# Where in a group of blocks the weight rounding stands: all of the group, or its first five sixths

## The chip, the cores and the metric

The program runs on one core of one Trainium2 chip. A core has five engines that work side by side, each through its own queue in order: TensorE (PE in the profile; its weight loads, which overlap its multiplications, are PEld), VectorE (DVE), ScalarE (ACT), GpSimd (POOL) and SyncE (SP), which here only issues transfers. The metric is the device time of one execution in microseconds (us), as the median of several runs. The kernel before took 2952.58 us (five runs, 2948.7 to 2953.84).

## The reference

```python
def _attn_ref(x, filt_r, filt_i):              # x: (8, 3008, 256)
    X = np.fft.rfft(x, axis=1)
    Y = X * (filt_r + 1j * filt_i)[None, :, :]
    return np.fft.irfft(Y, n=x.shape[1], axis=1).astype(np.float32)

def _moe_ref(x, w_gate, w_val, w_out):         # x: (24064, 256), d_ff = 1536
    g = x @ w_gate
    silu = g * (1.0 / (1.0 + np.exp(-g)))
    return (silu * (x @ w_val) @ w_out).astype(np.float32)
```

A filter in the frequency domain along the sequence is followed by a gated feed-forward block. The three weight matrices arrive in double precision, and the kernel turns them into single precision itself.

## The kernel before, in words

**Batches, groups, tokens.** The work goes through 8 batches. A batch is cut into 4 chunks of tokens, and the hidden dimension into 3 parts; one chunk with one part is a *group*, so a batch has 12 groups, counted 0 to 11 here. In the first batch groups 0 to 8 go part by part: chunks 0, 1, 2 with part 0, then with part 1, then with part 2. All groups walk through the same hand-written order, `SCHEDULE` (line 85), of 150 *tokens*; the position of a token is its *place*. Every engine takes its instructions in the order in which the tokens issue them. Tokens with a prime belong to the group before.

**What the tokens do.** The products x @ w_gate and x @ w_val are made by a scheme of block combinations. P, Q, A, B and E are products on PE (line 732; `P0` to `P3` and `Q0` to `Q3` with the blocks' own weights, `A01` to `E23` with combined ones). f and c copy a product out of PSUM (ACT, lines 747 and 751), D subtracts two such copies (POOL, `tensor_tensor` of line 228 with D as output), x, s and y combine products (DVE, lines 754 and 232; `x02`, `s12` and `s01` read `D02`, `D12` and `D01`). Of x03, x23 and x02 the s token is a copy on ACT (line 758). m copies (ACT, line 767), e and l go on (ACT line 763, DVE lines 228 and 232), g and u are the silu (ACT, line 774), h and v the product with it (DVE, line 779). The last token of a group, at place 149, is `v03`. S tokens (POOL, lines 225 and 228 with h) combine the hidden values of the group before, W tokens multiply them with the output weights (PE, line 811) and o tokens add the results up (ACT line 822, DVE line 225). t tokens are pieces of the transform of other chunks or of the next batch (lines 548 to 662). n1, n2 and n3 combine or fetch the sums of the next chunk's input blocks. `W2` is the first W token of a group, at place 3; it reads, among others, what `v03` wrote at the end of the group before, and output weights in `wo_t`.

**The preparation of the weights.** It happens once, in the first batch, since the weights are rounded from the raw 64-bit words by integer and floating-point instructions. There are 36 *halves*, each a 256 KB load by SP (line 285) and then (`round_half`, line 287) four DVE instructions (lines 302, 305, 317, 321), four ACT instructions (lines 307, 310, 312, 314) and one to five on POOL (line 329 and four subtractions of line 228 for output weights; lines 341 and 342 and up to two more for the others). After the halves of one part, `combine_weights` (line 351) makes the weights of A, B and E for six pairs, with one instruction on DVE, for some of them one on ACT (line 363), and two on POOL for each (lines 228 and 225 with `wt_t` or, for part 1, `lent`).

`Preparation` (line 378) cuts all of this into 171 *ticks*, numbered 0 to 170. A new half starts nearly every four ticks, and consecutive halves overlap. Within a half the steps come at ticks 0, 1, 2, 3, 4, 6, 7, 9 and 10 from its start: for instance L302 at 0, L305 at 1, L317 at 6, L321 at 7, the multiplication on POOL at 9, what follows it on POOL at 10. Calling `preparation.tick(step)` issues the instructions of the next tick, at this point of the order of every engine. Ticks 0 to 44 are done while the first chunk's transform runs, before group 0. After that the loop of line 1054 calls a tick just ahead of certain tokens:

```python
for place, token in enumerate(SCHEDULE):
    if b == 0 and this and place * TICKS % len(SCHEDULE) < TICKS and \
            (step or place > SCHEDULE.index("A01")):
        preparation.tick(step)
```

`TICKS` is 20 (line 451), so a group has 20 of them, and group 0 only those behind `A01`. At the start of each group `preparation.finish(step)` (line 1045) forces all ticks whose results that group needs: the output weights of part 0 are needed from group 1 on (tick 58 is their last), the weights of part 1 from group 3, those of part 2 from group 6, each with its output weights one group later. Ticks of part 2's weights, from 100 on, may not start before group 3, as they overwrite part 0's.

Of the kernel before, what the change touches and what calls it, by code (L numbers as in the profile page):

```python
# [84 lines left out]
SCHEDULE = """  # L85
# [59 lines left out]
def kernel(  # L145
# [228 lines left out]
    def reload_weights(g, piece):  # L374
        a, b = PIECES[piece]
        tc.keep_in_program_order(nc.sync.dma_start(out=wt_t[:, a:b], in_=w_dram[g, :, a:b]))
# [74 lines left out]
    TICKS = 20  # L451
# [388 lines left out]
    with tc.tile_pool(name="start", bufs=1) as spool0:  # L840
# [47 lines left out]
        for u in range(N_TWO + lag):  # L888
            if u < N_TWO:
                spec.turn(u + 2)  # L890
                step = spec.stage2a(u)
# [60 lines left out]
    def order_of(b):  # L952

        steps = [divmod(step, NG) for step in range(NCHUNK * NG)]
        if b == 0:
            steps[:NT * NG] = [(k, g) for g in range(NG) for k in range(NT)]
        return steps

    def sequence_of(cur, nxt, step):

        steps = order_of(cur.b)
        if step + 1 == len(steps):
            return (lambda d: combine_sequence(nxt.y[0], d)) if nxt else None
        k, after = steps[step][0], steps[step + 1][0]
        if k == after:
            return None
        if cur.b == 0 and NT - 2 < step < NT * NG - 1:
            return lambda d: reload_sums(after, d)
        return lambda d: combine_sequence(cur.y[after], d)

    def sooner(piece):

        for n in range(3):
            next(piece)
            if n == 2:
                next(piece, None)
            yield
# [24 lines left out]
    for b in range(B):  # L1002
        cur, nxt = spec, following if b + 1 < B else None
        spec, following = nxt, Spectral(b + 2)
        plan = [[] for _ in range(NCHUNK * NG)]

        def three(s, k, cur=cur):
            return [s.stage3(k, step) for step in range(4)]

        d = [three(cur, k) for k in range(1, NCHUNK)]  # L1010
        one = [nxt.stage1(u) for u in range(N_ONE)] if nxt else []
        two = []
        for u in range(N_TWO + 2) if nxt else ():
            two += [nxt.stage2b(u - 2)] if u > 1 else []
            two += [nxt.stage2a(u)] if u < N_TWO else []
        if nxt:
            plan[0] = one[0:2] + d[0][0:1] + one[2:3] + d[0][1:2]
            plan[1] = one[3:4] + d[0][2:3] + one[4:5] + d[0][3:4] + one[5:6]
            plan[2], plan[3] = one[6:11], one[11:16]
            plan[4] = d[1] + two[0:1]  # L1020

            plan[5], plan[6] = [iter(())] + two[1:5], two[5:10]
            plan[7] = two[10:11] + d[2]
            plan[8], plan[9] = two[11:16], two[16:21]
            plan[10], plan[11] = two[21:24], three(nxt, 0)
            if b == 0:
                for k in range(NCHUNK - 1):
                    plan[k] = d[k] + one[k:k + 1]
                plan[3], plan[4], plan[5] = one[3:8], one[8:13], one[13:16]
                for n in range(5):  # L1030
                    plan[6 + n] = two[5 * n:5 * n + 5]
                plan[6][0] = sooner(plan[6][0])
        else:
            plan[1], plan[4], plan[7] = d

        for step in range(NCHUNK * NG + (b == B - 1)):
            ghost = step == NCHUNK * NG
            k, g = order_of(b)[min(step, NCHUNK * NG - 1)]
            this = None
            pieces = []  # L1040
            if not ghost:
                pieces = plan[step]
                this = Group(b, k, g, cur.y[k], sequence_of(cur, nxt, step))
                if b == 0:
                    preparation.finish(step)
                chunk = {0: 1, 2: 2, 5: 3}.get(step)
                if b and chunk:
                    for i in range(2):
                        cur.load_t4(chunk, i)
            elif before is None:  # L1050
                break
            ends = {ORDER[e - 1]: n for n, (_, e) in enumerate(PIECES)}
            last = ghost or b == B - 1 and step == NCHUNK * NG - 1
            for place, token in enumerate(SCHEDULE):
                if b == 0 and this and place * TICKS % len(SCHEDULE) < TICKS and \
                        (step or place > SCHEDULE.index("A01")):
                    preparation.tick(step)
                old = token.endswith("'")
                op = token.rstrip("'")
                if op[0] == "t":  # L1060
                    n = int(op[1])
                    ps = pieces_before if old else pieces
                    if n < len(ps):
                        next(ps[n], None)
                elif op[0] in "Wo" or op.endswith(".o"):

                    g0 = older if old else before
                    if g0 is not None and (old or not ghost):
                        g0.project(op)
                else:  # L1070
                    g0 = before if old else this
                    if g0 is not None and not (ghost and op[0] == "S"):
                        g0.step(op)
                if old or this is None:
                    continue
                if nxt and (step, op) == ((4, "P2") if b else (5, "A23")):
                    nxt.load_two(0)
                if b + 2 < B and (step, op) == (9, "B01"):
                    for u in range(2):
                        following.load_x(u)  # L1080
                if nxt and (step, op) == (10, "A12" if b else "E23"):
                    for i in range(2):
                        nxt.load_t4(0, i)
                for f, args in chores.get((step, op), ()) if b == 0 else ():
                    f(*args)
                if op in ends and not last and (b or step >= NT * NG - 1):
                    reload_weights((g + 1) % NG, ends[op])
            older, before, pieces_before = before, this, pieces
# [33 lines left out]
```

## Time and profile before

| | |
|---|---|
| median of five runs | 2952.58 us |
| the profiled execution: its own time | 2952.58 us |
| its span, first to last instruction | 2950.2 us |
| mean granted PE clock | 0.999 |
| busy: PE / PEld / DVE / ACT / POOL | 99% / 95% / 65% / 55% / 54% |
| instructions on PE / DVE / ACT / POOL | 20264 / 4384 / 4208 / 1759 |
| groups 0 to 6 of the first batch (78.4 to 299.8 us): busy PE / DVE / ACT / POOL | 208.7 / 187.6 / 150.7 / 161.9 of 221.4 us |

In the timelines each line gives start and duration in us, the engine, the line of the code, the operation, output and inputs, their sizes and how many instructions the line stands for. A bracket at the end gives how long the engine was idle before it and what released it. Instructions of one engine overlap a little, so starts lie closer together than the durations. In the tables by stretch each engine has its busy time and, in brackets, its instructions; then come the granted PE clock, the DMA engines' busy share and GB/s. A wait for several things is put down to the one that came last.

### The profile page before, as it was taken

To read this page: it belongs to the slowest core of one execution; us is meant where nothing else is said; L and a number is where in the kernel's file an instruction comes from. 1 tells how busy PE (TensorE), PEld (TensorE's weight loads), DVE (VectorE), ACT (ScalarE), POOL (GpSimd) and SP (SyncE) were. 2 spreads that over 40 slices of the span, in tenths; PEclk is the share of its full clock that TensorE was granted. 3 is DMA by queue.
4 is the path that set the end of the run, shared out by engine and by line. 5 is a ranking of instruction groups with operands and counts; after the bars stand their busy time and mean duration, and the time that the engine had idled before them with its cause. 6 is when DMAs were issued, how large, how long until landed. Compare 5 with 4: busy or idle time off the path is not lost.

```text
span 2950.2 us, 57623 instructions
## 1 busy us (share of the span) xinstructions
PE 2913.9 (99%) x20264; PEld 2816.4 (95%) x20264; DVE 1930.8 (65%) x4384; ACT 1610.1 (55%) x4208; POOL 1579.3 (54%) x1759
## 2 busy tenths in 40 slices
PE   7999999999999999999999999999999999999999
PEld 5888999999999999999999999999999999999999
DVE  6888765576655776556765667656666566666666
ACT  6775455555555455555555554555555555555554
POOL 3875654556444655456554556454564545555453
PEclk9999999999999999999999999999999999999999
DMA  8687855575565755566655666556665565644442
GB/s 227 202 265 244 290 193 185 179 222 182 174 189 175 223 191 170 180 193 198 210 159 187 191 199 204 168 175 201 197 197 171 179 206 194 200 138 151 148 130 88
DMA packets 217452, 558.57 MB, mean 189 GB/s; under 512 B 29962, under 2 KB 107642, under 8 KB 217166
## 3 DMA queue, kind: packets, MB, share of 16 engines
q1 hardware_dynamic: 171326, 485.59, 52.2%
q10 hardware_dynamic: 36912, 45.43, 4.5%
q0 software_dynamic: 8928, 23.89, 2.3%
q8 instruction: 162, 2.65, 0.4%
q14 instruction: 124, 1.02, 0.1%
HBM read 459.73 MB, written 95.05 MB: 188 GB/s over the span
## 4 chain that ended last, share of the span: by engine, by line
PE 93%; DVE 1%; DMA 1%; POOL 1%; ACT 0%; issue 0%; SPq 0%; DVEq 0%
PE wa L732 24%; PE wA L811 17%; PE wk L732 16%; PE we L732 12%; PE wG L811 9%; PE wF L811 4%; PE pd L640 3%; PE pa L548 3%; PE pc L620 2%; PE pb L588 2%; DMA lent<-de_tbl 0%; DMA d<-lent 0%; DVE o L225 0%; POOL wt_t L225 0%; DVE pw L317 0%; POOL wt_t L228 0%
## 5 line engine op out<-in xcount | busy, mean ns | idle before, releaser
L732 PE MATMUL wa<-y_t,wt_t 128*128 128x188 f32 x4464 | 880.4, 323 | 5.3 <-issue 1.4
L732 PEld LDWEIGHTS wa<-y_t,wt_t 128*128 128x128 f32 x4464 | 730.0, 190 | 31.0 <-issue 17.3
L225 POOL TENSOR_TENSOR h<-h 128x376 f32<-128x376 f32 x190 | 182.9, 984 | 786.9 <-DVE h L779 767.7
L811 PE MATMUL wA<-wo_t,h 128*128 128x128 f32 x4608 | 577.8, 275 | 3.0 <-DVE o L225 2.0
L811 PEld LDWEIGHTS wA<-wo_t,h 128*128 128x128 f32 x4608 | 563.0, 192 | 16.9 <-issue 10.4
L732 PE MATMUL wk<-y,wt_t 128*128 128x188 f32 x2976 | 568.5, 324 | 0.0
L228 POOL TENSOR_TENSOR h<-h 128x376 f32<-128x376 f32 x570 | 554.4, 994 | 0.5
L732 PEld LDWEIGHTS wk<-y,wt_t 128*128 128x128 f32 x2976 | 479.7, 191 | 25.9 <-issue 19.8
L228 DVE TENSOR_TENSOR we<-we,m 128x376 f32<-128x376 f32 x576 | 318.4, 556 | 197.3 <-PE we L732 138.9
L732 PE MATMUL we<-y_t,wt_t 128*128 128x188 f32 x2232 | 431.5, 323 | 1.4 <-ACT we L763 1.4
L732 PEld LDWEIGHTS we<-y_t,wt_t 128*128 128x128 f32 x2232 | 369.4, 190 | 1.8 <-ACT we L763 1.7
L228 POOL TENSOR_TENSOR D<-f,f 128x376 f32<-128x376 f32 x288 | 280.5, 987 | 104.3 <-ACT f L747 103.3
L232 DVE SCALAR_TENSOR_TENSOR y<-wk,c 128x376 f32<-128x376 f32 x480 | 244.8, 542 | 133.4 <-ACT we L763 82.8
L767 ACT COPY m<-wa 128x376 f32<-128x376 f32 x576 | 272.0, 472 | 88.0 <-PE wa L732 86.8
L774 ACT ACTIVATE g<-wa 128x188 f32<-128x188 f32 x576 | 188.1, 327 | 190.3 <-PE wa L732 182.3
L811 PE MATMUL wG<-wo_t,h 128*128 128x128 f32 x2304 | 288.3, 275 | 0.6 <-DVE o L225 0.6
L811 PEld LDWEIGHTS wG<-wo_t,h 128*128 128x128 f32 x2304 | 281.4, 192 | 0.8 <-DVE o L225 0.8
L774 ACT ACTIVATE u<-we 128x188 f32<-128x188 f32 x576 | 189.0, 328 | 168.8 <-DVE we L228 150.0
L747 ACT ACTIVATE f<-wk 128x376 f32<-128x376 f32 x288 | 139.3, 484 | 235.3 <-PE wk L732 208.0
L751 ACT COPY c<-wk 128x376 f32<-128x376 f32 x288 | 136.0, 472 | 225.3 <-PE wk L732 225.3
L754 DVE SCALAR_TENSOR_TENSOR x<-wk,f 128x376 f32<-128x376 f32 x192 | 104.3, 543 | 235.6 <-PE wk L732 229.9
L763 ACT COPY we<-y 128x376 f32<-128x376 f32 x480 | 224.1, 487 | 33.6 <-DVE h L779 14.8
(142 smaller groups left out, 3914.8 us busy)
## 6 DMA issues: line engine op xcount, KB each, us to landing
wt_t<-w_all SPq DMA_DIRECT2D x174, 896.0 KB
wt_t<-w_all SPq DMA_DIRECT2D x174, 768.0 KB
t<-d SPq DMA_DIRECT2D x62, 384.0 KB
d<-t ACTq DMA_DIRECT2D x112, 192.0 KB
lent<-de_tbl SPq DMA_DIRECT2D x84, 256.0 KB
lent<-in_filt_r_dram SPq DMA_DIRECT2D x336, 64.0 KB
lent<-d SPq DMA_DIRECT2D x84, 256.0 KB
d<-lent ACTq DMA_DIRECT2D x84, 256.0 KB
```

What stands on the lines that cost most here:

```text
L225: return eng.tensor_tensor(out=dst, in0=a, in1=b, op=ALU.add)
L228: return eng.tensor_tensor(out=dst, in0=a, in1=b, op=ALU.subtract)
L232: return nc.vector.scalar_tensor_tensor(out=dst, in0=a, scalar=-1.0, in1=b, op0=ALU.mult, op1=ALU.subtract)
L548: pin(nc.tensor.matmul(out=ps[0:NK], lhsT=wf_t, rhs=self.x.pop(u), start=True, stop=True))
L732: pin(nc.tensor.matmul(out=ps[:, z], lhsT=self.wt[:, SLOT[p], z], rhs=rhs, start=start and z == 0, stop=True, skip_group_check=True))
L747: pin(act.mul(self.small(f"f{i}", f"f{i}", 1), t[f"k{i}"], -1.0))
L751: pin(act.copy(out=self.small(f"c{i}", f"c{i}", 1), in_=t[f"k{i}"]))
L754: pin(v.scalar_tensor_tensor(out=dst, in0=t[f"k{j}"], scalar=-1.0, in1=t[f"f{i}" if j == 3 else f"D{at}"], op0=ALU.mult, op1=ALU.add))
L763: pin(act.copy(out=self.bank(f"e{at}"), in_=t[f"y{at}"]))
L767: pin(act.copy(out=self.small(f"m{at}", "m", 4), in_=t[f"a{at}"]))
L774: pin(act.activation(out=self.small(op, "g", 3, 1)[:, 0], in_=ps[:, 1], func=AF.Silu))
L811: pin(nc.tensor.matmul(out=self.tiles[at][:, t, :], lhsT=self.hs[i][:, HID[p], t0:t0 + 128], rhs=wo_t[:, JB * q + i, WO[p], :], start=star ...
```

## The change

The ticks are spread over the places ahead of `E01` (place 127) instead of over all 150, still 20 in a group, and in group 0 they begin behind `P0` (place 27) instead of behind `A01` (place 52). Nothing else is altered: the ticks, what each of them issues, and the forced ones at the starts of groups are the same.

```diff
             for place, token in enumerate(SCHEDULE):
-                if b == 0 and this and place * TICKS % len(SCHEDULE) < TICKS and \
-                        (step or place > SCHEDULE.index("A01")):
+
+                span = SCHEDULE.index("E01")
+                if b == 0 and this and place < span and place * TICKS % span < TICKS and \
+                        (step or place > SCHEDULE.index("P0")):
                     preparation.tick(step)
```

## The prediction

> **What bounds the kernel now.** I read the page's busy table first, then busy time by stretch, then the timelines of PE, POOL and DVE in the one stretch where PE has idle time.
>
> ```profile
> PE 2913.9 (99%) x20264; PEld 2816.4 (95%) x20264; DVE 1930.8 (65%) x4384; ACT 1610.1 (55%) x4208; POOL 1579.3 (54%) x1759
> ```
>
> ```profile
> 0.00:78.40 78.40, 62.85 (x328) 46.85 (x328) 53.95 (x103) 48.69 (x96) 28.50 (x43) 0.98 0.89 229
> 78.40:299.80 221.40, 208.68 (x1383) 194.17 (x1383) 187.57 (x406) 150.70 (x415) 161.86 (x210) 0.99 0.72 235
> 299.80:2950.20 2650.40, 2642.35 (x18556) 2575.40 (x18555) 1689.26 (x3876) 1410.72 (x3698) 1388.90 (x1507) 1.00 0.58 184
> ```
>
> The columns are stretch, its length, then busy time of PE, PEld, DVE, ACT and POOL, granted clock, DMA share and GB/s. PE is the bound. The rounding that the change moves lies in the middle row alone, groups 0 to 6 of the first batch (they start on PE at 78.4, 104.2, 141.2, 174.4, 206.4, 236.6 and 267.8). There PE is idle for 221.40 - 208.68 = 12.7 us: no reordering in it can gain more than that and a slow clock, below.
>
> Where it waits is in PE's timeline (idle and releaser in brackets): W2 of group 1, at the very start of that group, then A01 in group 1, E03 in group 2, and W2 of group 3.
>
> ```profile
> 107.80 1.38 PE L811 MATMUL wF<-wo_t,h 128*128 128x128 f32 x10 [2.59 <-POOL wo_t L329]
> ...
> 120.20 1.54 PE L732 MATMUL wa<-y_t,wt_t 128*128 128x188 f32 x8 [0.43 <-DVE wa L754]
> ...
> 169.52 0.91 PE L732 MATMUL we<-y_t,wt_t 128*128 128x188 f32 x4 [1.40 <-ACT we L763]
> ...
> 176.91 1.38 PE L811 MATMUL wF<-wo_t,h 128*128 128x128 f32 x10 [1.52 <-DVE h L779]
> ```
>
> The longest wait is followed by a slow clock (third number from the end: 0.67, 0.50, 0.50, 0.62), which costs 0.33 + 0.50 + 0.50 + 0.38 = 1.7 us more.
>
> ```profile
> 109.00:110.00 1.00, 1.00 (x9) 1.00 (x8) 0.00 (x0) 0.00 (x0) 1.00 (x4) 0.67 0.71 185
> 110.00:111.00 1.00, 1.00 (x5) 1.00 (x5) 0.00 (x0) 0.40 (x1) 1.00 (x2) 0.50 0.50 181
> 111.00:112.00 1.00, 1.00 (x5) 1.00 (x5) 0.00 (x0) 0.74 (x3) 1.00 (x2) 0.50 0.99 356
> 112.00:113.00 1.00, 1.00 (x6) 1.00 (x6) 0.00 (x0) 0.79 (x2) 1.00 (x3) 0.62 1.01 388
> ```
>
> The last sixths of groups 0, 2 and 3 (4.7 us each) show what the change empties: DVE 4.45, 4.39 and 4.16 busy, full.
>
> ```profile
> 99.40:104.10 4.70, 4.69 (x26) 4.19 (x27) 4.45 (x10) 4.19 (x12) 4.54 (x6) 1.00 0.32 80
> ...
> 169.70:174.40 4.70, 4.70 (x31) 4.17 (x32) 4.39 (x9) 3.02 (x11) 3.34 (x5) 1.00 0.64 206
> 201.70:206.40 4.70, 4.70 (x32) 4.19 (x30) 4.16 (x13) 4.11 (x13) 0.30 (x1) 1.00 1.00 363
> ```
>
> **The change part by part.** No instruction is added or removed. By counting places in the order of 150 tokens: a group's 20 ticks go from 7.5 places apart (0 to 143) to about 6.35 (0 to 121). In group 0, 13 ticks (45 to 57, places 53 to 143) become 15 (45 to 59, places 32 to 121). From then on every group is one tick ahead, a tick comes 1.5 us (slot 1) to 5.8 us (slot 0) earlier, and the rounding ends at place 64 of group 6 instead of 83. Tick 58, forced at the start of group 1, is now inside group 0.
>
> *Group 0, POOL's queue.* D02 and D12 stand at places 48 and 51. Before, tick 45 comes after them; now ticks 45 and 46 come before. POOL's timeline shows what they issue:
>
> ```profile
> 84.92 2.87 POOL L228 TENSOR_TENSOR D<-f,f 128x376 f32<-128x376 f32 x3
> 87.75 0.78 POOL L228 TENSOR_TENSOR wt_t<-wt_t 128x256 f32<-128x256 f32 x1
> 88.49 0.91 POOL L225 TENSOR_TENSOR wt_t<-wt_t 128x256 f32<-128x256 f32 x1
> 89.36 0.73 POOL L329 TENSOR_TENSOR wo_t<-wo_t,pw 128x256 f32<-128x256 f32 x1
> 90.04 0.73 POOL L228 TENSOR_TENSOR wt_t<-wt_t 128x256 f32<-128x256 f32 x1
> 90.73 0.91 POOL L225 TENSOR_TENSOR wt_t<-wt_t 128x256 f32<-128x256 f32 x1
> ```
>
> The last five (87.75 to 91.61, 3.86 us) now precede the second and third D, so D02 ends at 85.9 + 3.86 + 0.96 = 90.7. DVE needs it for x02:
>
> ```profile
> 88.73 0.54 DVE L754 SCALAR_TENSOR_TENSOR x<-wk,D 128x376 f32<-128x376 f32 x1
> ```
>
> So x02 slips by 2.0, and behind it on DVE y12, y02, h13 and s12, for which A12 on PE waits (from 91.9 to about 93.8). Against this, DVE's rounding after x02 falls from 6.6 us (L302, L305, L317 and L321 rows from 90.10 to 104.57) to 6.1: L321 at 90.10, L302 at 91.70 and L305 at 93.24 leave, L317 and L321 of ticks 58 and 59 (0.33, 0.87 at the rows from 106.75) arrive. DVE's idle time from there to v03 is 0.74 + 0.25, which a late DVE no longer has. v03 ended at 106.83, so it now ends at 106.83 + 2.0 - 0.5 - (0 to 1.0) = 107.3 to 108.3.
>
> *W2 of group 1* needs v03 and wo_t. The wo_t product (L329 at 106.78, tick 57, place 143) moves to place 108, ahead of n2 and n1 on POOL, and so leaves the path: late next is v03. W2 goes from 107.80 to about 107.85 (-0.45 to +0.55; at best, if DVE isn't late, -2.59). I take 0.
>
> *The clock.* The wait ahead of W2 shrinks anyway, because PE already waits at A12: from 2.6 to between 0.8 (s03 slips as well) and 2.4 (it doesn't). Waits of 1.40 and 1.52 left the clock at 1.00, 2.59 did not; 1.6, the middle, is nearer to 1.52. I take -1.7, the other end is 0. [...]
>
> *Group 1, DVE.* The three waits at A01 and after (0.43, 0.47, 0.18) come from a rounding instruction held on DVE:
>
> ```profile
> 114.04 3.92 DVE L317 SCALAR_TENSOR_TENSOR pw<-wo_t,pw 128x256 uint32<-128x256 uint32 x1
> ```
>
> It moves from place 23 to 13, ahead of x03 and s13, into DVE's idle 4.43 us before 113.12. Gone: -1.08. If it is held there until POOL's run ends (117.7 instead of 113.1), A13 waits some 3 us: +2.0. No other rounding instruction on DVE between 78 and 300 took over 1.7, so I take -0.8.
>
> *Group 2.* From x02 (154.43) to v03 (176.86) DVE is idle for 0.69 in all: it sets both waits. Rounding and combinations on DVE behind x02 fall from 11.9 to 11.1 (out L302 0.65 and L305 0.56 at 155.81 and 157.09, in L321 0.41 at 176.78), while one add (0.46 at 155.30) passes D02. I take -0.4; ends -3.35 (all waits of groups 2 and 3) and +0.46. The denser ticks only shift the wait forward inside the group.
>
> *Group 3.* Four subtractions (188.09, 2.0 us) pass D02; POOL starts 0.55 earlier, D02 had 1.29 of slack: 0.16 is left; I take 0, at most +0.7.
>
> *Group 5.* One pair of combinations more precedes D01 and all six precede D02. POOL runs without a gap from 236.29 to 256.6 there, and DVE already waits:
>
> ```profile
> 252.44 0.55 DVE L754 SCALAR_TENSOR_TENSOR x<-wk,D 128x376 f32<-128x376 f32 x1 [1.56 <-POOL D L228]
> ```
>
> The pair that passes D02 took 253.32 to 254.69, 1.4 us; less PE's small waits just after (0.4), +1.0. Ends 0 and +1.4.
>
> *Groups 4 and 6, ACT and SP.* A single add of 0.45 passes D02 (group 4), nothing in group 6: 0. ACT's rounding keeps its order to DVE's; its idle time is over 5 us in each of groups 0 to 6. The raw loads (256 KB each) stand up to 5.8 us earlier in SP's queue, past keeps and reloads; the only PE wait on a DMA here or soon after is 0.69 at 351.8, so -0.7 to +0.7, taken as 0.
>
> A rounding L302 took 0.28 at 263.54, with POOL idle, and 1.24 at 102.88 under a POOL instruction. POOL is nearly idle in the last sixths of groups 3 to 5 (0.30 in the row above), which rounding now leaves; 4 instructions times 0.96 in 3 groups is 11.5 us of DVE, against 4.7 + 5.6 + 3.1 of its idle time: hidden, 0. [...]
>
> Sum: 0 - 1.7 - 0.8 - 0.4 + 0 + 1.0 = -1.9. The profiled execution took 2952.58 (span 2950.2 and 2.4 around it), which is also the median of the five: 2952.58 - 1.9 = 2950.7.
>
> **The rivals.** *A, the end waits go.* DVE without rounding in the last sixth finishes v03 with PE: 2.59, the clock's 1.7, 1.08 and 1.52 leave: -6.9, 2945.7. For it: DVE full in those sixths. Against: x02 restarts DVE late, and the rounding behind it hardly shrinks.
>
> *B, slower: POOL's queue in front of D02.* The engine that decides is POOL: what passes D02 is 3.86 in group 0 (2.0 beyond x02), 0.45 in groups 1, 2 and 4, 2.0 in group 3, and in group 5 1.4. It decides if DVE has no idle time left behind x02 and PE pays in full: 2.0 + 1.4 + 2.0 + 1.4 = 6.8 with the clock's stretch still slow and nothing won elsewhere: 2959.4. Against: the idle time in group 0 and the slack in group 3.
>
> *C, nothing:* gains and losses within 0.5, 2952.6, with the clock dipping as before.
>
> **How the numbers follow.** Forecast 0.52, A 0.20, B 0.16, C 0.12. 0.2% (5.9 us) is about what a measurement of this kernel can tell from no change. Faster by more is A and a little of the forecast's favourable ends, 0.22; slower by more is B and a new clock dip of 1.7 on top of unfavourable ends, 0.17; within, 0.61. Favourable ends together give -8.7; the unfavourable ones +5.1. The range takes A in and reaches close to B: 2944.5 to 2958.5.
>
> **What would show it.** Right: POOL's five wt_t and wo_t instructions between D01 and D02 in group 0, x02 near 90.7, W2 of group 1 released by DVE h instead of POOL wo_t and near 107.8, clock 1.00 from 109 to 113, L317 ahead of 113, W2 of group 3 near 176.5, x02 of group 5 waiting some 3 us. Wrong: v03 of group 0 near 105.5 (A), or a second clock dip, or waits on POOL D in groups 1 to 4 (B). From 330 us on the two traces should differ by a constant.

## The result and the profile after

The changed kernel takes 2956.45 us (median of 25 runs, 2955.15 to 2964.17); the kernel before, run beside it, takes 2949.18 us (45 runs, 2947.25 to 2955.02). The ratio is 1.0024, with a 95% interval of 1.0018 to 1.0029: **slower, by about 7 us**. The forecast was 2950.7, 1.9 faster than the profiled execution of before. 2956.45 lies inside the range, but on the other side of no change.

The profiled execution of the changed kernel took 2956.77 us, its span 2954.8. First the busy line and busy time by stretch, with the columns used above (stretch, length, PE, PEld, DVE, ACT, POOL, clock, DMA share, GB/s):

```profile
PE 2915.1 (99%) x20264; PEld 2817.8 (95%) x20264; DVE 1932.8 (65%) x4384; ACT 1613.0 (55%) x4208; POOL 1581.0 (54%) x1759
```

```profile
0.00:78.40 78.40, 62.88 (x336) 47.48 (x337) 54.98 (x105) 49.80 (x99) 28.47 (x43) 0.98 0.89 231
78.40:299.80 221.40, 205.37 (x1344) 190.32 (x1344) 185.19 (x396) 150.41 (x407) 161.89 (x208) 0.98 0.71 231
299.80:2950.20 2650.40, 2646.83 (x18588) 2580.04 (x18586) 1692.50 (x3885) 1412.77 (x3705) 1390.64 (x1508) 1.00 0.58 184
```

The instructions are as many as before on every engine. In the middle stretch PE is idle for 16.0 us where it was 12.7, and the mean clock falls from 0.99 to 0.98. From the end of group 6 to the end of the span it is 2650.5 us here and 2650.6 in the execution shown of before: all of the loss lies in groups 0 to 6.

To find it, I measured each group as the time from its first matrix product (`Q0`) on PE to the next group's. *Before, again 1* and *2* are two more executions of the kernel before, and *after, again* is one of the changed kernel:

| us | start | group 0 | 1 | 2 | 3 | 4 | 5 | 6 |
|---|---|---|---|---|---|---|---|---|
| before, shown above (2952.58) | 78.43 | 25.73 | 37.07 | 33.14 | 32.03 | 30.24 | 31.13 | 31.84 |
| before, again 1 (2949.99) | 78.41 | 25.74 | 35.22 | 34.44 | 30.35 | 30.24 | 30.46 | 31.86 |
| before, again 2 (2951.38) | 78.17 | 25.76 | 35.21 | 32.74 | 32.03 | 30.24 | 30.46 | 31.86 |
| after (2956.77) | 77.30 | 28.28 | 33.60 | 39.98 | 30.47 | 30.24 | 32.55 | 31.91 |
| after, again (2956.64) | 77.90 | 28.32 | 33.61 | 38.91 | 30.49 | 30.24 | 32.55 | 31.91 |

Against *before, again 1*, the changed kernel's groups 0 and 1 together cost 0.9 more, groups 2 and 3 together 5.7 more (4.6 in its other execution), group 4 nothing, group 5 costs 2.1 more, group 6 nothing: 8.7 in all, of which a start that is 1.1 earlier takes off some (that start varied from 77.3 to 80.1 over the executions of this study, without order, and was 85.5 in `hold2`, whose granted clock was 0.76 from 60 to 80 us). In these profiles group 2 is the largest part; what it is worth in the medians follows below.

**Group 2.** PE's timeline there:

```profile
160.76 0.90 PE L732 MATMUL wa<-y_t,wt_t 128*128 128x188 f32 x4 [2.12 <-ACT m L767]
...
166.43 0.90 PE L732 MATMUL we<-y_t,wt_t 128*128 128x188 f32 x4 [0.94 <-DVE we L232]
...
171.39 1.03 PE L732 MATMUL wa<-y_t,wt_t 128*128 128x188 f32 x4 [2.08 <-POOL wo_t L228]
```

Two waits of over 2 us (`B02`, `A03`; the middle one is `E13`) stand where before there was one of 1.4 (at `E01`, place 127; the prediction calls that product E03). Both are followed by a slow clock, as the stretches show (0.67 and 0.70; each time the granted clock is 0.50 for 3.41 us, together 3.4 us of PE time lost):

```profile
160.00:165.00 5.00, 4.24 (x19) 4.24 (x20) 3.91 (x9) 3.22 (x10) 4.00 (x7) 0.67 0.63 239
...
170.00:175.00 5.00, 3.61 (x13) 3.61 (x14) 3.45 (x10) 3.77 (x10) 2.27 (x5) 0.70 0.78 277
```

Follow the first wait back, from ACT to DVE to POOL:

```profile
159.52 0.42 ACT L307 ACTIVATE w<-w 128x256 f32<-128x256 uint32 x1 [2.00 <-DVE w L302]
159.84 0.47 ACT L763 COPY we<-y 128x376 f32<-128x376 f32 x1
160.24 0.47 ACT L767 COPY m<-wa 128x376 f32<-128x376 f32 x1
```

```profile
158.68 0.80 DVE L302 TENSOR_SCALAR w<-wo_t 128x256 uint32<-128x256 uint32 x1 [1.30 <-POOL lent L225]
```

```profile
155.91 2.33 POOL L228 TENSOR_TENSOR h<-h 128x376 f32<-128x376 f32 x2
158.18 0.47 POOL L225 TENSOR_TENSOR lent<-w,lent 128x128 f32<-128x128 f32 x1
158.59 0.74 POOL L228 TENSOR_TENSOR lent<-lent 128x256 f32<-128x256 f32 x1
```

POOL does S30 and S31 (line 228 with h) before the last addition of an earlier half (158.18). Only that addition frees the `w` buffer which L302 of the next half writes, so DVE stands for 1.30. ACT's rounding step L307 needs L302 and stands for 2.00, with m02 (160.24) behind it in ACT's queue; PE needs m02 for `B02`. The second wait has the same form. The profile names POOL as its releaser, but that instruction writes output weights that `A03` does not read; what ended last is the copy `s03`, at 171.29 on ACT, behind a rounding step that waits for a late DVE:

```profile
170.41 0.51 ACT L310 ACTIVATE pw<-pw,off_t 128x256 f32<-128x256 uint32 x1 [1.07 <-DVE pw L305]
170.82 0.47 ACT L758 COPY wa<-x 128x376 f32<-128x376 f32 x1
```

And in the last sixth, which the change empties of rounding, DVE now waits for PE:

```profile
173.71 0.56 DVE L228 TENSOR_TENSOR we<-we,m 128x376 f32<-128x376 f32 x1 [0.21 <-PE we L732]
174.96 0.56 DVE L228 TENSOR_TENSOR we<-we,m 128x376 f32<-128x376 f32 x1 [0.70 <-PE we L732]
177.39 0.56 DVE L228 TENSOR_TENSOR we<-we,m 128x376 f32<-128x376 f32 x1 [1.12 <-PE we L732]
```

**DVE's own price.** The groups of DVE instructions by line show L302 in group 2 of the changed kernel (count, then total us and mean ns, then idle time before):

```profile
L302 DVE TENSOR_SCALAR w<-wo_t 128x256 uint32<-128x256 uint32 x3 | 3.3, 1097 | 1.3 <-POOL lent L225 1.3
...
L302 DVE TENSOR_SCALAR wo_t<-raw 128x256 uint32<-128x256 uint32 x1 | 1.1, 1076 | 0.0
L302 DVE TENSOR_SCALAR w<-raw 128x256 uint32<-128x256 uint32 x1 | 1.1, 1056 | 1.1 <-POOL lent L225 1.1
...
L302 DVE TENSOR_SCALAR wo_t<-wo_t 128x256 uint32<-128x256 uint32 x1 | 0.8, 817 | 0.0
```

and in group 2 of *before, again 2*:

```profile
L302 DVE TENSOR_SCALAR wo_t<-wo_t 128x256 uint32<-128x256 uint32 x1 | 0.8, 815 | 0.0
L302 DVE TENSOR_SCALAR w<-raw 128x256 uint32<-128x256 uint32 x1 | 0.6, 642 | 0.0
L302 DVE TENSOR_SCALAR w<-wo_t 128x256 uint32<-128x256 uint32 x2 | 0.6, 284 | 0.0
L302 DVE TENSOR_SCALAR wo_t<-raw 128x256 uint32<-128x256 uint32 x1 | 0.5, 543 | 0.0
```

The same instruction takes 1.04 us on average (six, 6.2 us; one of them begins 0.25 us ahead of the group) where it took 0.51 (five, 2.6 us). All six begin while a POOL instruction runs. What it pays can be read from the rows above: the L302 that begins at 158.68, under POOL's instruction of 158.59, ends at 159.48, 0.15 after that instruction. It is so throughout the first 320 us of the traces of *before* and *after* shown here: of 72 instances of L302, 39 took over 0.35 us (16 in *before*, 23 in *after*); each of these began while a POOL instruction ran and ended 0.15 to 0.16 us after one. The other 33 took 0.27 to 0.30: 31 began with POOL free, 2 in the last 0.1 us of a POOL instruction.

**Group 5** is longer by 2.1. PE's timeline:

```profile
251.78 1.51 PE L732 MATMUL wa<-y_t,lent 128*128 128x188 f32 x8 [0.68 <-PE wk L732]
253.64 0.49 PE L811 MATMUL wA<-wo_t,h 128*128 128x128 f32 x2 [0.35 <-POOL h L228]
254.58 1.38 PE L811 MATMUL wA<-wo_t,h 128*128 128x128 f32 x10 [0.45 <-POOL h L228]
...
259.75 1.60 PE L811 MATMUL wA<-wo_t,h 128*128 128x128 f32 x12 [0.87 <-DVE o L225]
```

PE's idle time in the group is 2.35 us against 0.93 in *before, again 2*, and its products take 0.67 more busy time. What is behind it is `x02`, which waits for POOL's D02 for 3.63 us on DVE (it was 1.56), and POOL's S results, which W tokens on PE wait for twice.

**Groups 0 and 1.** In group 0 PE waits 1.06 at `A12` and 1.89 at `A03` (before: not at all and 1.40), and then only 0.30 at W2, where it waited 2.59:

```profile
92.91 0.90 PE L732 MATMUL wa<-y_t,wt_t 128*128 128x188 f32 x4 [1.06 <-DVE wa L754]
...
100.82 0.88 PE L732 MATMUL wa<-y_t,wt_t 128*128 128x188 f32 x4 [1.89 <-POOL y_t L225]
...
106.90 1.35 PE L811 MATMUL wF<-wo_t,h 128*128 128x128 f32 x10 [0.30 <-DVE h L779]
...
123.07 0.90 PE L732 MATMUL wa<-y_t,wt_t 128*128 128x188 f32 x4 [0.72 <-ACT wa L758]
...
133.09 0.88 PE L732 MATMUL wa<-y_t,wt_t 128*128 128x188 f32 x4 [0.80 <-POOL y_t L225]
```

and the slow clock behind W2 is gone:

```profile
105.00:110.00 5.00, 4.70 (x36) 4.54 (x35) 4.67 (x7) 2.82 (x8) 4.92 (x5) 1.00 0.94 309
110.00:115.00 5.00, 5.00 (x39) 5.00 (x38) 4.57 (x8) 3.53 (x12) 4.92 (x7) 1.00 0.76 273
```

Yet from W2's resumption to the end of group 1 it is 32.28 us, and 31.57 in *before, again 2*, which has the slow clock. New waits (0.72, 0.80) took its place.

### The profile page after: what moved, and what is told of

It reads as the page before. It is cut to its first block, busy times and chain, and to the rows that moved or that the text cites. A ratio compares the mean times of both kernels' runs of the same rounds, so it can differ in the third digit from the quotient of the medians.

```text
span 2954.8 us, 57634 instructions
## 1 busy us (share of the span) xinstructions
PE 2915.1 (99%) x20264; PEld 2817.8 (95%) x20264; DVE 1932.8 (65%) x4384; ACT 1613.0 (55%) x4208; POOL 1581.0 (54%) x1759
## 4 chain that ended last, share of the span: by engine, by line
PE 93%; POOL 2%; DMA 2%; DVE 1%; ACT 1%; issue 0%; SPq 0%; ACTq 0%; POOLq 0%; DVEq 0%
PE wa L732 24%; PE wA L811 17%; PE wk L732 16%; PE we L732 12%; PE wG L811 9%; PE wF L811 4%; PE pd L640 3%; PE pa L548 3%; PE pc L620 2%; PE pb L588 2%; DMA f<-in_filt_i_dram 0%; POOL y_t L225 0%; DMA y_t<-yt 0%; POOL h L228 0%; POOL D L228 0%
```

## The experiments

The theory after the result: the loss is group 2's, by the order of queues just shown (the `w` buffer behind POOL's S, ACT's rounding steps ahead of m02 and s03); group 5's is POOL's weight combinations ahead of D02. The rivals: the amount of DVE's work in the squeezed stretch with L302's doubled price, whatever the order; and a chance difference between two single executions.

### The two kernels again

Two more executions of the kernel before:

> The kernel before, unaltered, for a second trace of it: its median (2949) lies 3.4 us under the profiled execution shown. If the slow clock behind W2 of group 1 comes and goes, a trace near 2949 has the same waits on PE and no slow clock at 109 to 113 (groups 0 and 1 together 61 instead of 62.8 us). If it is always there, the 3.4 us lie elsewhere, ahead of group 0 or after group 6.

> The kernel before, unaltered, for a third trace, to the same end as the second.

They are the second and third rows of the table. Groups 0, 4 and 6 agree within 0.03 us; the execution that the prediction was made from stands apart in group 1 (37.07 against 35.2) and group 5 (31.13 against 30.46). Its three waits at A01 and behind it and its L317 of 3.92 us occur in neither. The slow clock behind W2 is there in both (mean clock of group 1 0.95 in each, as in the execution shown), so it does not make the difference. The same for the changed kernel:

> The changed kernel, unaltered, for a second trace. Its runs lie close together (half of them within 2955.5 to 2956.8), so the waits in group 2 with their two slow clocks should be there again: group 2 between 39 and 41 us. If one slow clock is missing, some 38, and then part of the 3 us that each experiment saved is chance.

2956.64 us, with the same groups within 0.1, but for group 2 (38.91). Group 2 again has 6.8 us of slow clock, now in one piece, and its waits are 2.11 at `B02`, 0.92 at `B12` and 1.44 at `E13`, with none at `A03`. Chance differences between executions are 1 to 2 us in groups 1 to 3; they do not make 5.

### Group 2 alone

The changed kernel with the old spacing in group 2 (`g2old`):

```diff
-                span = SCHEDULE.index("E01")
+                span = len(SCHEDULE) if step == 2 else SCHEDULE.index("E01")
```

> The changed kernel, with group 2 alone on the old spacing (its ticks 80 to 99 at places 0 to 143). Theory G2 (the loss lies in group 2: there the denser rounding and the combinations of part 1 make PE wait twice for over 2 us, and each wait slows the clock): group 2 shrinks from 40.0 us to 33 to 35, the clock stays at 1.00 between 155 and 180, and the kernel ends 1 us under to 1 us over the kernel before (ratio 0.9995 to 1.0005). Rival D (POOL work that now passes D02 in groups 0 and 5 is what is paid): nothing of it is touched, ratio 1.0015 to 1.0025.

The kernel before with the new spacing in group 2 alone (`g2new`):

```diff
+                span = SCHEDULE.index("E01") if step == 2 else len(SCHEDULE)
-                if b == 0 and this and place * TICKS % len(SCHEDULE) < TICKS and \
+                if b == 0 and this and place < span and place * TICKS % span < TICKS and \
```

> The kernel before, with group 2 alone on the new spacing (ticks 79 to 98 at places 0 to 121). Theory G2: the loss comes back with this part alone, group 2 takes 38 to 40 us with two stretches of slow clock, ratio 1.0015 to 1.0025. Rival D: no change, ratio 0.9995 to 1.0005.

`g2old`: 2953.53, ratio 1.0019 [1.0009, 1.0028]; groups 2 and 3 take 64.6 (33.72 + 30.88), as in the kernel before (64.8). `g2new`: 2951.84, ratio 1.0012 [1.0003, 1.0020]; groups 2 and 3 take 67.5 (37.22 + 30.25), with 6.8 us of slow clock in group 2 (3.4 us lost), and every other group is as before. Its PE timeline in group 2:

```profile
162.66 0.90 PE L732 MATMUL wa<-y_t,wt_t 128*128 128x188 f32 x4 [1.27 <-ACT m L767]
165.28 1.62 PE L732 MATMUL we<-y_t,wt_t 128*128 128x188 f32 x4 [1.72 <-DVE we L232]
```

These are `B12`, which waits for m12 on ACT, and `E13`: the waits begin one product later than `B02`. So in the profiles the loss is bound to the spacing in group 2: it goes with it and comes with it.

In the times the theory missed. `g2old` was expected back at the kernel before (0.9995 to 1.0005), and its 1.0019 lies in the range of rival D; its profiled execution, 2952.20, was the fastest of its eleven. `g2new` came out below the theory's range (from 1.0015), and its interval reaches down to the rival's (up to 1.0005). By the medians the spacing in group 2 is worth 2.9 us (2956.45 against 2953.53) or 3.0 (2951.84 against 2948.8 beside it) of 7.3, and 4.7 remain without it. Of these the profiles show 2.1 in group 5 and 0.9 in groups 0 and 1; some 1.7 are not placed. In the profiled executions `g2new` loses 2.7 in groups 2 and 3, the changed kernel 4.6 to 5.7; the changed kernel is a tick further on when it comes to group 2, but that this makes the difference was not tried.

### The order of the queues in group 2

A third place for `w`, borrowed from output weights that lie idle, for halves 15 and 21, so that L302 of halves 21 and 22 finds its buffer free (`wspare`):

```diff
+        elif i in (15, 21):
+            w = wo_t.rearrange("p j i f -> p (j i f)")[:, 3200:3456]
+            w = w.rearrange("p (b f) -> p b f", b=2)
```

> The changed kernel, with a buffer of its own (unused room in the output weights' tile) for the mantissas of halves 15 and 21, so that L302 on DVE no longer waits for POOL to release one: in the changed kernel it waited 1.10 and 1.30 us in group 2. Theory W (that wait is what holds DVE, then ACT's L307, then m02, then B02 on PE): the wait of 2.12 before B02 falls under 0.7 and its slow clock goes, group 2 takes 35 to 37.5 us, ratio 1.0008 to 1.0016. Rival L (DVE has too much to do in this stretch anyway, and the wait only fills time): within 1 us of the changed kernel, ratio 1.0020 to 1.0027.

The ticks of places 83 and 115 put behind m02 and s03 (`behind`):

```diff
+                    if step == 2:
+                        moved = {83: 86, 115: 116}
+                        here = here and place not in moved or place in moved.values()
```

> The changed kernel, with two ticks of group 2 a few places later: the one of place 83 at 86 (behind m02 instead of ahead of it) and the one of place 115 at 116 (behind s03). Theory Q (a rounding instruction on ACT that waits for DVE stands in the queue ahead of m02 and of s03, for which B02 and A03 on PE wait): both PE waits (2.12 and 2.08) fall under 1, no slow clock in group 2, which takes 34 to 36 us, ratio 1.0003 to 1.0012. Rival L (DVE is late with everything in this stretch): both waits stay over 1.5 us, ratio 1.0018 to 1.0027.

Five of DVE's final rounding instructions left out (`light`):

```diff
-        pin(v.scalar_tensor_tensor(out=w.rearrange(flat), ...
+        if i not in range(19, 24):
+            pin(v.scalar_tensor_tensor(out=w.rearrange(flat), ...
```

> The changed kernel, with L321 (the adding of the low words on DVE, 0.4 to 0.95 us each) left out in halves 19 to 23, so that these weights lack their low bits: the order of all queues stays, DVE has about 3 us less to do in group 2. Theory L (DVE is overloaded between places 64 and 121 of group 2): the PE waits of 2.12, 0.94 and 2.08 fall to under 2.5 in all, at most one slow clock, group 2 takes 35 to 37 us instead of 40, ratio to the kernel before 1.0010 to 1.0017. Rival Q (it is the order of the queues, ACT's rounding ahead of m02 and s03 and DVE's wait for POOL): the waits stay at 4.5 or more, ratio 1.0021 to 1.0027.

The first two together (`both`), and all three (`all3`):

> The changed kernel with the spare buffer for the mantissas of halves 15 and 21 and with the two ticks of group 2 behind m02 and s03, together. Each alone took 3 us off group 2 (40.0 to 37.0), with one slow clock left. If the order of the queues is the whole of group 2's loss, both together bring it to 34 to 35 with no slow clock, ratio 1.0006 to 1.0012. If DVE's load is what remains, group 2 stays at 36 to 37 with a wait of some 2 us on DVE or ACT somewhere between B02 and E03, ratio 1.0012 to 1.0017.

> The same, and L321 left out in halves 19 to 23 (these weights lack their low bits; some 3 us less for DVE). If DVE's load and the order of the queues are together the whole loss of group 2: 33 to 34.5, no slow clock, ratio 1.0004 to 1.0010 (the rest being groups 0, 1 and 5). If something else holds PE there: 35 or more.

| | group 2 | groups 2 + 3 | PE time lost to the clock in group 2 | median, us | ratio to before |
|---|---|---|---|---|---|
| after (two executions) | 39.98, 38.91 | 70.4, 69.4 | 3.4, 3.4 | 2956.45 | 1.0024 [1.0018, 1.0029] |
| `wspare` | 37.01 | 67.5 | 1.7 | 2956.47 | 1.0029 [1.0018, 1.0039] |
| `behind` | 37.00 | 67.5 | 1.7 | 2954.33 | 1.0016 [1.0007, 1.0025] |
| `light` | 36.21 | 66.7 | 1.7 | 2954.66 | 1.0015 [1.0006, 1.0024] |
| `both` | 36.36 | 66.8 | 1.7 | 2954.24 | 1.0015 [1.0006, 1.0023] |
| `all3` | 34.46 | 64.9 | 0 | 2951.45 | 1.0004 [0.9995, 1.0012] |
| before (again 1, 2) | 34.44, 32.74 | 64.8, 64.8 | 1.7, 0 | 2949.18 | 1 |

Each remedy alone takes 2 to 4 us off group 2, and half of its slow clock with it. In the median that shows for `behind` and `light` (some 2 us), not for `wspare` (7 runs), where `B02` still waits 1.50 (under 0.7 was expected). `behind` did what it was made for: `B02` and `A03` wait no more. But the tick moved to place 86 and the one of place 89 still stand ahead of m12 (place 91), and PE now waits 1.95 at `B12` and 2.13 at `E13`, so that the group takes 37.0 and not 34 to 36. In `both` it is the same: L302 no longer waits for the buffer, and m02 and s03 no longer stand behind those steps, but PE waits at `B12` and `E13`:

```profile
162.61 0.90 PE L735 MATMUL wa<-y_t,wt_t 128*128 128x188 f32 x4 [1.76 <-ACT m L770]
165.58 1.39 PE L735 MATMUL we<-y_t,wt_t 128*128 128x188 f32 x4 [2.06 <-DVE we L232]
```

(lines are shifted by 3 here, and by up to 4 in `all3`). On ACT, m12 (at 162.10) stands behind three instructions that waited for DVE, two rounding steps and the silu g3:

```profile
158.98 0.42 ACT L310 ACTIVATE w<-w 128x256 f32<-128x256 uint32 x1 [0.59 <-DVE w L305]
160.09 0.33 ACT L777 ACTIVATE g<-wk 128x188 f32<-128x188 f32 x1 [0.70 <-DVE y L232]
...
161.69 0.51 ACT L313 ACTIVATE pw<-pw,off_t 128x256 f32<-128x256 uint32 x1 [0.38 <-DVE pw L308]
```

`E13` waits for e13, DVE's own result; DVE has no idle time there from 156.2 to 167.3, and the L302 instances still take 0.8 to 1.5 us each. So `both` took two waits in the queues away, and another that is in part of the same kind came up: it does not separate the order of the queues from DVE's lateness. Only with the five DVE instructions taken out as well do the waits fall to 1.2 and less (the two longest are shown), and groups 2 and 3 to the length of before:

```profile
161.28 0.91 PE L736 MATMUL wa<-y_t,wt_t 128*128 128x188 f32 x4 [0.72 <-ACT m L771]
163.39 0.91 PE L736 MATMUL we<-y_t,wt_t 128*128 128x188 f32 x4 [1.20 <-DVE we L232]
```

So group 2's loss goes when the three remedies come together. That the queues' order is a part of it is shown by `behind` (the two waits that it aimed at went), and that DVE's work is a part by `light` and `all3`; how much is each was not separated. The amount of DVE's rounding alone does not decide: lines 302, 305, 317 and 321 take 11.8 us in group 2 of *before, again 2*, 14.3 in the changed kernel, 13.8 in `g2old`, whose group 2 takes 33.72, and 11.6 in `light`, whose group 2 takes 36.21.

### POOL's queue in groups 0 and 5

The POOL part of the ticks is kept back until D02 and D12 are issued (the kernel has `hold` and `release` for it), in groups 0 and 5 of the changed kernel (`hold`), and the same with group 2's old spacing (`hold2`):

```diff
+                held = b == 0 and step in (0, 5) and (30 if step == 0 else 25) < place <= 51
+                if b == 0 and step in (0, 5) and this and place == 52:
+                    preparation.release()
...
+                elif here and not (held and place == 51):
+                    preparation.tick(step, hold=held)
```

> The changed kernel, with POOL's part of the ticks held back in group 0 (places 32 to 45) and group 5 (places 26 to 45) until D12 (place 51) is issued; the tick of place 51 stands at 52 there. Rival D (POOL work that passes D02 in groups 0 and 5 is a part of the loss): x02 waits for D no more, group 5 goes from 32.55 to 31.0 to 31.3 us, groups 0 and 1 together lose 0.5 to 1.5, ratio against the kernel before 1.0012 to 1.0020 (the changed kernel: 1.0024). Theory G2 alone: 1.0022 to 1.0027.

> The same hold, and group 2 on its old spacing as well. If group 2 and POOL's work ahead of D02 are the whole loss, this ends with the kernel before or below it: ratio 0.9990 to 1.0005. If there is a third cause, 1.0007 or more stays.

`hold`: 2953.93, ratio 1.0012 [1.0003, 1.0022]; group 5 takes 28.89 instead of 32.55, group 0 29.80 instead of 28.28, with a slow clock (1.7 us lost) in it that the two executions of the changed kernel have not. Groups 0 and 1 together take 62.9 against 61.9, where 0.5 to 1.5 less was expected: in group 0 the hold did not pay in this execution. `hold2`: 2950.71, ratio 1.0006 [0.9997, 1.0014]; group 2 is 33.74, group 5 28.89. With group 2 and group 5 undone, the change can't be told from no change. But group 5 is 1.6 below before there, and the median still 1.3 above the kernel before beside it (2949.45), so by this estimate some 3 us lie elsewhere. The profile shows 1.4 of them in groups 0 and 1 (62.4 against 61.0), in an execution whose granted clock was 0.86 from 78 to 107 us; the rest is not placed.

Group 5 falls below the 30.46 of before, so the combinations ahead of D02 were paid for in the kernel before too. The next run takes the hold alone, in the kernel before (`hold5`):

```diff
+                if here:
+                    preparation.tick(step, hold=step == 5 and 14 < place <= 51)
+                if b == 0 and step == 5 and this and place == 52:
+                    preparation.release()
```

> The kernel before, with POOL's part of the combinations in group 5 held back until D12 is issued (they stand behind D01, D02 and the S instructions then). In the hold of the changed kernel group 5 took 28.9 us against 30.5 before the change. If POOL's combinations ahead of the D instructions are what group 5 pays, it goes from 30.5 to 28.7 to 29.3 here too: 2947.3 to 2948.3, ratio 0.9993 to 0.9997. If not, 1.0000.

2946.43 us (2945.62 to 2948.31), ratio 0.9988 [0.9979, 0.9997]: a little faster than both kernels, and more so than expected. Group 5 takes 28.51 us, and in the 28.5 us from 234.00 on PE is busy throughout. On POOL the D instructions now come when their inputs do, and the combinations after them:

```profile
238.56 0.98 POOL L228 TENSOR_TENSOR D<-f,f 128x376 f32<-128x376 f32 x1 [0.96 <-ACT f L747]
...
242.79 1.99 POOL L228 TENSOR_TENSOR D<-f,f 128x376 f32<-128x376 f32 x2 [1.19 <-ACT f L747]
244.74 0.73 POOL L228 TENSOR_TENSOR wt_t<-wt_t 128x256 f32<-128x256 f32 x1
```

### The slow clock at W2

`hold5`, and in group 0 the tick of place 143 called at 138, so that the product for wo_t stands ahead of n1 on POOL (`best1`):

```diff
+                if b == 0 and step == 0 and place in (138, 143):
+                    here = place == 138
```

> The same, and the last tick of group 0 at place 138 instead of 143, so that POOL multiplies the last output weights of part 0 ahead of n1 (three instructions, 4.1 us) instead of behind it. By the prediction's step on W2 v03 is late next there: W2 at 106.9 instead of 107.8 and a PE wait of about 1.7 instead of 2.59; with the slow clock behind it as before, ratio 0.9989 to 0.9994, and without it 0.9983 to 0.9988. If W2 waits for something else, as hold5.

2946.87 us, ratio 0.9993 [0.9984, 1.0002]: no better than `hold5`, where 0.9983 to 0.9988 was expected without the slow clock. W2's wait falls from 2.59 to 1.08 (0.26 + 0.82), and there is no slow clock. But group 1 is 34.32 instead of 35.20, only 0.9 shorter for 1.5 us of wait and 1.7 us of clock. New waits show where it went:

```profile
105.82 1.35 PE L811 MATMUL wF<-wo_t,h 128*128 128x128 f32 x10 [0.82 <-DVE h L779]
116.67 1.54 PE L732 MATMUL wa<-y_t,wt_t 128*128 128x188 f32 x8 [0.57 <-DVE wa L754]
118.78 1.58 PE L811 MATMUL wA<-wo_t,h 128*128 128x128 f32 x12 [0.57 <-ACT o L822]
```

A PE that is sooner done with its first products of group 1 only waits sooner for DVE.

## Why the prediction was wrong

**The step that failed is "Group 2 ... I take -0.4", with its sentence that the denser ticks only shift the wait forward inside the group.** Measured: +4.6 to +5.7 with group 3 in the two profiles of the changed kernel, and 2.9 to 3.0 in the medians of `g2old` and `g2new`, all outside the ends of -3.35 and +0.46. The other terms together were forecast at -1.5; with group 2 on its old spacing (`g2old`) the median is 4.7 above before, so the rest of the sum failed too: its favourable terms (the clock, group 1) brought nothing, group 5 cost twice its term, and some 1.7 us are not placed. The step counted the rounding *behind x02 on DVE* and found less of it. It did not go through the queues that the denser ticks run into: L302 waits for a buffer that POOL frees behind S30 and S31, ACT's L307 and L310 stand ahead of m02 and s03, and the lateness cannot be made good at the end, because DVE then waits for PE (0.21, 0.70, 1.12). The prediction had the row that speaks for it: DVE idle for 0.69 us in all between x02 and v03. With so little slack DVE had nothing to make a wait good with.

**The price of L302** was taken as hidden, 0. It went from 0.51 to 1.04 us in group 2, 2.6 to 6.2 us with one instance more, and `light` and `all3` show that DVE's load there counts. The weighing looked at the last sixths of groups 3 to 5 only. What the rows show of it is its form: L302 ended 0.15 to 0.16 us after a POOL instruction in all 39 long instances of the two traces; why it does, no run here shows.

**Group 0, POOL's queue: right.** x02 stands 12.39 us after the start of its group (89.69 - 77.30) where it stood 10.30: +2.1, predicted +2.0. W2 resumes 29.60 after the start, 29.37 before: +0.2, predicted +0.05. DVE h releases it, as predicted. The wait left for W2 is 0.30, not 0.8 to 2.4: PE comes to the end of group 0 later than foreseen (28.28 instead of 25.74), for besides `A12` it waits longer at `A03` (1.89 instead of 1.40), behind ACT's rounding, and 0.3 each at `P2` and `A02`.

**The clock, -1.7: the event right, its worth wrong.** The clock was 1.00 behind W2. Groups 0 and 1 together nevertheless cost 0.9 more. `best1`, which removes the same slow clock in another way, points to the reason: PE's lost time was mostly hidden behind DVE.

**Group 1, -0.8: a term that priced one execution.** The held L317 and its waits do not recur in two further executions of the kernel before. (It ended at 117.96, 0.28 after the last of the POOL instructions that ran one behind another until 117.68; in *again 1* the same L317 began at 114.03, took 0.68 and came to its end behind the first of them.) The profiled execution took 2952.58, 3.4 above the median of 45 runs, and was also the median of the five shown, so nothing in the numbers at hand said so.

**Group 3, 0: right** to about a us: 30.47 and 30.49, against 30.35 and 32.03. The wait of W2 that comes in some executions of before (*again 2* has it, *again 1* has not) is gone in both executions, but paid for by group 2.

**Group 5, +1.0: right in mechanism and sign, too small:** +2.1, above its upper end of 1.4. The x02 term was about right (16.99 us after the group's start against 15.82: +1.2), and x02's wait of 3.63 near the 3 foreseen. Left out was what else is behind the combinations on POOL, the S results (0.35 and 0.45 of wait on PE).

**Groups 4 and 6 and the rest: right,** 0.0, 0.0 and a constant from there on.

**The rivals.** A is refuted: W2's waits did go (2.59 to 0.30, and 1.52 to none), and the kernel became slower. B had the sign, and POOL's queue in front of D02 decides in group 5; in groups 1 to 4 of the changed kernel DVE has no wait on D, and group 2's part came through another queue.

## What to carry to other kernels

When background work is moved closer together, walk through each queue that it enters and look for the foreground instruction that stands right behind it, and for the buffer whose release lies on another engine; a count of the work on one engine sees neither. Capacity emptied at the end of a stage is of no use if the stage's own dependences keep the engine waiting there. Take several executions of the kernel before where the terms are 1 to 2 us, and before counting a stall of one engine as a gain, ask which engine has no slack behind it.

## What the runs showed of the hardware

The clock fell after shorter waits of PE than the rows of before suggested (1.40 and 1.52 without, 2.59 with). In group 2, *before, again 1* has a slow clock after a wait of 1.41 (mean clock of the group 0.95), *again 2* none after 1.39 (1.00):

```profile
167.28 1.62 PE L732 MATMUL we<-y_t,wt_t 128*128 128x188 f32 x4 [1.41 <-ACT we L763]
```

At `A03` in group 0, a wait of 1.91 was followed by a slow clock in `g2old` (0.75 from 100 to 105 us) and one of 1.91 was not in `both` (1.00); one of 2.69 was in `light` (0.70) and one of 2.69 was not in `wspare` (1.00). So in these runs the length of one wait, between 1.4 and 2.7 us, did not decide.

In the clock records of *before* and *after*, each slow clock but the last, which the end of the trace cuts off, lasts 3.41 us at 0.50; by that it takes up to 1.7 us from PE, an estimate. They start at 34.26, 109.35 and 2949.24 in *before* and at 32.03, 161.73, 171.97 and 2953.83 in *after*, in each trace a whole number of 3.413 us apart (22 and 854; 38, 41 and 856 after the first). In `g2new` the clock was 0.94, 0.50 and 0.88 in the three stretches of 5 us from 160 to 175: slow for some 6.8 us, an estimate. In the 3.41 us ahead of a slow clock PE was busy for 1.29, 1.55 and 0 us in *before*, and for 0.48, 1.31, 1.33 and 0 in *after*. Of the other stretches of 3.413 us at full clock, counted on from the first slow one, the least busy had 1.49 in *before* (68.39 to 71.80) and 1.64 in *after* (55.92 to 59.33), and the clock behind them was 1.00. The two executions of group 2 above had PE busy for 1.57 and for 1.78 us in such a stretch, the one that holds the wait or most of it:

```profile
163.90:167.32 3.42, 1.57 (x10) 1.27 (x9) 3.42 (x9) 1.40 (x4) 3.42 (x6) 1.00 0.96 255
167.32:170.73 3.41, 3.41 (x8) 2.29 (x9) 3.41 (x7) 1.98 (x6) 3.01 (x4) 0.50 0.51 211
...
163.42:166.84 3.42, 1.78 (x11) 1.28 (x9) 3.42 (x9) 1.40 (x4) 3.42 (x6) 1.00 0.98 250
166.84:170.25 3.41, 3.23 (x17) 2.70 (x18) 3.41 (x7) 2.21 (x7) 3.23 (x4) 1.00 0.65 251
```

So the clock fell behind 1.55 and 1.57 us of busy PE and less, and not behind 1.49, 1.64 and 1.78. That goes with the busy time better than with the length of one wait, but 1.49 stands against it; what decides, no run here shows.

A small instruction on DVE (L302, 128x256, uint32) took from 0.27 to 1.47 us in the first 320 us of *before* and *after*: where it took over 0.35 (39 of 72), it had begun under a POOL instruction and ended 0.15 to 0.16 us after one.
